# Retention in half chunks: q and k laid out over the partitions by halves, scores and state products in one stretch of TensorE, outputs in one stretch

## The chip, the core and the metric

The kernel runs on one core of a Trainium2 chip. The metric is the device time in microseconds (us), median of three runs. The engines are TensorE (PE, with its weight loads PEld), VectorE (DVE), ScalarE (ACT), GpSimd (POOL) and SyncE (SP), which issues all the loads and stores here.

## The reference

A retention layer (linear attention with a decay per head) feeds a two-layer network with an ELU. All is fp32.

```python
# q, k, v: (B, H, S, D) = (4, 8, 768, 64); gamma[h] = 1 - 2 ** (-5 - h)
for t in range(S):
    state = gamma * state + k[:, :, t] (outer) v[:, :, t]
    y[:, :, t] = scale * q[:, :, t] @ state
x = y.transpose(0, 2, 1, 3).reshape(3072, 512)
h = x @ w_in                                   # 512 -> 2048
out = where(h > 0, h, exp(min(h, 0)) - 1) @ w_out   # 2048 -> 512
```

Retention is a small part of the arithmetic; the two products with w_in and w_out are the rest.

## The kernel before

The 3072 tokens are cut into 24 chunks of 128 and these into 6 blocks (`tb`) of 512. For each block the kernel computes the retention of its 4 chunks, which gives x transposed in `xb`, and then two phases of the network: the first phase (x times w_in, with ELU into tiles `gC`, `gT`) and the second (times w_out). Block 0 uses plain products (`plain_first` L455, `plain_second` L483); later blocks use Strassen's scheme, partly twice nested (`first_twice` L733, `first_rest` L786, `second_twice` L813), with 128x128 and 128x256 matmuls whose sums and differences VectorE and ScalarE form. Some weights are decoded on VectorE during block 0 (`prepare` L140, `decode` L167), combined and stored to scratch memory, and fetched from there in the second phases (`fetch_small` L675).

The order of every engine's work is written out by hand: the program text interleaves the retention of block tb+1 with the phases of block tb. The function `retention_step` (L1065) is called at chosen places: in the main loop (L1127) steps 1 and 0 stand in the first phase (L1187, L1204) and steps 2 to 4 in the second (L1217). For block 2 all steps lie in block 1's second phase (L1121); for block 1 they lie between the matmuls of `plain_second` (L1046 to L1056); for block 0 everything is at the start (L983 to L1033), part by part as the loads land.

Retention works on half chunks of 64 tokens, `sub` = 0 or 1, and a state is a 64x64 matrix per head. Decay is folded into v (`scale_v` L258, on POOL for most chunks: v' = v times a factor per token and head) and into a factor per token at the end (`etab`). So a state is the plain running sum of k^T v', and the output of a half chunk is (masked scores) times v' plus q times the state in front of it. All these matmuls are 64x64x64: each uses one of four quarters of the PE array, given by the half of the partitions that the operands lie on (row half) and the half of the partitions of the output (column half).

Before the change q and k lie transposed, with the head pairs on the partition halves: tile `qk` is [64*a + d, q or k, head pair p, token of the chunk], head = 2p + a. Token-major k and v lie in `kvn` [token, k or v, head, d]. Then:

- `scores` (L299) computes the scores of two chunks: row half a (the head parity), column half sub, bank `sc[a]`. VectorE multiplies by the causal mask (L305) and writes into the k^T part of `qk`.
- `states` (L339): k^T v' of each half chunk in row half sub, column half a, bank `kvs[sub]`; `state_sum` (L330) adds it to the state before on VectorE (128 partitions x 256), or copies it on ScalarE where a sequence starts. States are kept in the place of k in `kvn`; the last of a block goes to `carry`.
- `outputs` (L348), a generator with pauses, accumulates y in two banks `y[sub]`. The products with the masked scores (L363) use row half sub. Those with the state (L389) use row half a, in two rounds: first where a = sub, then where a differs from sub. In the second round a row half writes into the bank that the other row half has just written, so two small reads of the banks on VectorE (`seen`, L377) stand between the rounds, and matmuls of the second wait for them. Then VectorE multiplies by `etab` into `xb` (L398).

Per block the 64x64 matmuls stand in five places of TensorE's order: all scores; all state products; L363 and the first round of outputs for chunks 0 and 1; the same for chunks 2 and 3; the second round of both.

The pool `ps_r` has four PSUM banks, taken in turn by `sc`, `kv`, `y` and two products of the first phase. The first phase's sums (`first_end` L799, add at L802) read PSUM on VectorE; TensorE then accumulates a further product into the same bank (L794).

Of the kernel before, what the change touches and what calls it, by code (L numbers as in the profile page):

```python
# [17 lines left out]
def kernel(  # L18
# [85 lines left out]
    def load_one(m, which, behind=None):  # L104
        if which == 0:
            raw[m] = [ldpool.tile([P, 2, HP, C], FP32, name="qk", tag="qk"), None]
            t = raw[m][0].rearrange("p a h c -> p (a h c)")
        else:
            raw[m][1] = ldpool.tile([C, 2, H, D], FP32, name="kvn", tag="kvn")
            t = raw[m][1].rearrange("p a h c -> p (a h c)")  # L110
        hold(t, behind)
        nc.sync.dma_start(t, qkv[m, :, 1024 * which : 1024 * which + 1024])
# [142 lines left out]
    carry = [const.tile([P, HP, D], FP32, name=f"carry{n}") for n in range(2)]  # L255
# [18 lines left out]
    def state(tb, n):  # L274

        if n % (2 * CPB) == 0:
            return carry[(tb + n // (2 * CPB)) % 2]
        if (tb, n) == (0, 3):

            return xt[0].rearrange("p a t -> p (a t)")[:, 0:256].rearrange("p (h e) -> p h e", e=D)  # L280

        k = raw[tb * CPB + (n - 1) // 2][1][:, 0].rearrange("p h d -> p (h d)")
        return k[:, (n - 1) % 2 * 256 : ((n - 1) % 2 + 1) * 256].rearrange("p (h e) -> p h e", e=D)
# [5 lines left out]
    def score_products(sc, tb, pp, x):  # L289
        qk = raw[tb * CPB + 2 * pp + x][0]  # L290
        for p in range(HP):
            for sub in range(2):
                for a in range(2):
                    nc.tensor.matmul(  # L294
                        sc[a][rows(sub), x, p, :], lhsT=qk[rows(a), 1, p, rows(sub)],
                        rhs=qk[rows(a), 0, p, rows(sub)], start=True, stop=True, skip_group_check=True,
                    )

    def scores(tb, pp):  # L299

        sc = [ps_r.tile([P, 2, HP, D], FP32, name="sc", tag="r") for _ in range(2)]
        for x in range(2):
            score_products(sc, tb, pp, x)
        for a in range(2):
            nc.vector.tensor_tensor(  # L305
                out=raw[tb * CPB + 2 * pp + a][0][:, 1].rearrange("p h c -> p (h c)").rearrange("p (n t) -> p n t", t=D),
                in0=sc[a].rearrange("p x h t -> p (x h) t"),
                in1=cmask.unsqueeze(1).to_broadcast([P, 2 * HP, D]), op=ALU.mult,
            )

    def mask_pair(sc, x):

        place = raw[x][0][:, 1].rearrange("p h c -> p (h c)").rearrange("p (a n t) -> p a n t", a=2, t=D)
        for a in range(2):
            nc.vector.tensor_tensor(
                out=place[:, a], in0=sc[a][:, x], in1=cmask.unsqueeze(1).to_broadcast([P, HP, D]), op=ALU.mult
            )

    def state_products(kvs, tb, pp, x, subs):
        kv = raw[tb * CPB + 2 * pp + x][1]  # L320
        for p in range(HP):
            for sub in subs:
                for a in range(2):
                    if not fresh(tb, 4 * pp + 2 * x + sub + 1):
                        nc.tensor.matmul(  # L325
                            kvs[sub][rows(a), x, p, :], lhsT=kv[rows(sub), 0, 2 * p + a, :],
                            rhs=kv[rows(sub), 1, 2 * p + a, :], start=True, stop=True, skip_group_check=True,
                        )

    def state_sum(kvs, tb, pp, x, sub):  # L330
        n = 4 * pp + 2 * x + sub
        if fresh(tb, n + 1):
            return
        if fresh(tb, n):
            nc.scalar.copy(state(tb, n + 1), kvs[sub][:, x])
        else:
            nc.vector.tensor_tensor(out=state(tb, n + 1), in0=kvs[sub][:, x], in1=state(tb, n), op=ALU.add)

    def states(tb, pp):  # L339

        kvs = [ps_r.tile([P, 2, HP, D], FP32, name="kv", tag="r") for _ in range(2)]
        for x in range(2):
            state_products(kvs, tb, pp, x, range(2))
        for x in range(2):
            for sub in range(2):
                state_sum(kvs, tb, pp, x, sub)

    def outputs(tb, pp, first=False):  # L348
# [6 lines left out]
        for x in range(2):  # L355
            kv = raw[tb * CPB + 2 * pp + x][1]
            for j in range(4):
                a, u = divmod(j, 2)
                pt = raw[tb * CPB + 2 * pp + (x if first else a)][0][:, 1].rearrange("p h c -> p (h c)")
                for sub in range(2):  # L360
                    for c in range(2):
                        p = 2 * u + c
                        nc.tensor.matmul(  # L363
                            y[sub][rows(c), j, x, :], lhsT=kv[rows(sub), 1, head(a, u, c), :],
                            rhs=pt[rows(sub), ((a if first else x) * HP + p) * D :][:, 0:D],
                            start=(x == 0 and j == 0), stop=False, skip_group_check=True,
                        )
            if first and x == 0:
                yield
        for other in range(2):  # L370
            if not other:
                yield
            else:

                for sub in range(2):
                    seen = epool.tile([P, 8], FP32, name="seen", tag="seen")
                    nc.vector.tensor_copy(seen.rearrange("p (j x) -> p j x", x=2), y[sub][:, :, :, 0])  # L377
                yield
            for x in range(2):
                q = raw[tb * CPB + 2 * pp + x][0]  # L380
                for u in range(2):
                    for a in range(2):
                        sub = a ^ other
                        n = 4 * pp + 2 * x + sub
                        if fresh(tb, n):
                            continue
                        for c in range(2):
                            p = 2 * u + c
                            nc.tensor.matmul(  # L389
                                y[sub][rows(c), 2 * a + u, x, :], lhsT=state(tb, n)[rows(a), p, :],  # L390
                                rhs=q[rows(a), 0, p, rows(sub)], start=False, stop=True, skip_group_check=True,
                            )
        if first:
            yield
# [8 lines left out]
    def outputs_step(tb, step):  # L403

        if step == 0:
            held["y"] = [outputs(tb, pp) for pp in range(2)]
        if step < 2:
            next(held["y"][step])
            next(held["y"][step])
        else:  # L410
            for g in held["y"]:
                next(g, None)
# [569 lines left out]

    unread(2, TB)  # L983
    sc = [ps_r.tile([P, 2, HP, D], FP32, name="sc", tag="r") for _ in range(2)]
    score_products(sc, 0, 0, 0)
    mask_pair(sc, 0)
    scale_v(0)
    unread(1, TH)
    kvs = [ps_r.tile([P, 2, HP, D], FP32, name="kv", tag="r") for _ in range(2)]
    state_products(kvs, 0, 0, 0, range(2))  # L990
    state_sum(kvs, 0, 0, 0, 0)
    state_sum(kvs, 0, 0, 0, 1)
# [5 lines left out]
    score_products(sc, 0, 0, 1)  # L998
    take(2)
    mask_pair(sc, 1)  # L1000
# [4 lines left out]
    state_products(kvs, 0, 0, 1, [0])  # L1005
    next(y)
    state_sum(kvs, 0, 0, 1, 0)
# [3 lines left out]
    next(y)  # L1011
    take(2)
    next(y)
    state_products(kvs, 0, 0, 1, [1])
# [3 lines left out]
    state_sum(kvs, 0, 0, 1, 1)  # L1018
# [6 lines left out]
    scores(0, 1)  # L1025
    states(0, 1)
# [19 lines left out]
    for n, _ in enumerate(plain_second()):  # L1046
        decode_all()
        prepare()
        if n == 1:
            scores(1, 0)  # L1050
            scores(1, 1)
        elif n == 2:
            states(1, 0)
            states(1, 1)
        elif 3 <= n <= 5:
            outputs_step(1, n - 3)  # L1056
        elif n == 6:
            for _ in combine_w_in(0):
                pass
# [3 lines left out]


    def retention_step(tb, step):  # L1065
        if tb >= NTB:
            return
        if step == 0:
            scores(tb, 0)
            scores(tb, 1)  # L1070
        elif step == 1:
            states(tb, 0)
            states(tb, 1)
        elif step < 5:
            outputs_step(tb, step - 2)
# [43 lines left out]
    for step, s in enumerate(sec):  # L1119
        if step in (0, 1, 2, 4, 5):  # L1120
            retention_step(2, (0, 1, 2, 2, 3, 4)[step])  # L1121
        if s == ORDER2[-1]:
            break
# [3 lines left out]
    for tb in range(2, NTB):  # L1127
# [86 lines left out]
        for step, s in enumerate(sec):  # L1214

            if step in (1, 3, 5):
                retention_step(tb + 1, 2 + step // 2)  # L1217
# [54 lines left out]
```

## Time and profile before

| what | value |
|---|---|
| device time, median of 3 runs | 648.82 us (647.68 to 651.66) |
| span of the profiled execution, first to last instruction | 645.3 us |
| PE busy | 634.9 us, 98% of the span |
| VectorE busy | 496.9 us, 77% |
| ScalarE busy | 240.8 us, 37% |
| POOL busy | 39.0 us, 6% |
| mean granted TensorE clock | 0.997 |
| scores L294: PE instructions, duration of one | 768, 218 ns |
| state products L325 | 704, 218 ns |
| products with masked scores L363 | 704 and 64 (block 0's first), 218 ns |
| mask L305, 128x512 | 22, 680 ns |
| state sum L337, 128x256 | 30, 425 ns (10 more in groups of other operands) |
| first state of a sequence, ScalarE L335, 128x256 | 4, 373 ns |
| `seen` L377, 128x8 | 24, 158 ns |
| outputs times etab L398, 128x512 | 24, 680 ns |

The profile is of one execution, of which only the span is recorded and no device time; the median of the runs is 3.5 us above the span. Matmuls of different array quarters overlap, and their ends are modelled, so the duration of one says little about the pace: that is read from when groups start. Idle time of an engine is given with what ended it; "issue" means that nothing in the profile explains it. A few records of matmuls are missing from the trace, so that counts in a stretch can be a little low.

In time, block 0's start and plain products take up to about 145 us of the span (the retention of block 1 at 94 to 131 us), block 1 up to about 250 us (the retention of block 2 at 199 to 242), and each of blocks 2 to 5 about 100 us.

### The profile page before, as it was taken

How to read it: one execution, taken by the hardware profiler on the slowest of the kernel's cores; microseconds unless marked ns; L12 is line 12 of the kernel's file. 1: busy time of each engine (PE TensorE's matmuls, PEld its weight loads, DVE VectorE, ACT ScalarE, POOL GpSimd, SP SyncE). 2: the span in 40 equal slices, each digit the busy share in tenths (PEclk: the TensorE clock that was granted, in tenths of full speed). 3: DMA queues.
4: the chain of work that ended last, by engine and by line, in shares of the span. 5: the costliest groups of instructions: out<-in, count | busy, mean ns of one | idle time of the engine just before them, and what ended most of it. 6: DMA issues, size and time to landing. Idle time of an engine off the chain costs nothing.

```text
span 645.3 us, 15896 instructions
## 1 busy us (share of the span) xinstructions
PE 634.9 (98%) x6526; PEld 542.7 (84%) x6526; DVE 496.9 (77%) x889; ACT 240.8 (37%) x463; POOL 39.0 (6%) x41
## 2 busy tenths in 40 slices
PE   7999999999999999999999999999999999999998
PEld 4774445548889999989999989999988999988998
DVE  4889799898979676589867488867569959557976
ACT  4577531204552112556111465211465311356311
POOL 1001100000460000100000110000020000000000
PEclk9999999999999999999999999999999999999999
DMA  8749777999488789802789920788840688710695
GB/s 302 288 136 369 267 236 213 319 272 258 150 282 268 211 262 316 294 5 56 245 278 289 306 87 16 223 275 286 292 171 3 197 263 264 226 49 1 212 313 162
DMA packets 85209, 139.72 MB, mean 217 GB/s; under 512 B 6672, under 2 KB 38800, under 8 KB 82832
## 3 DMA queue, kind: packets, MB, share of 16 engines
q1 hardware_dynamic: 85136, 138.70, 66.5%
q8 instruction: 52, 0.85, 0.5%
q14 instruction: 21, 0.17, 0.1%
HBM read 114.56 MB, written 24.12 MB: 215 GB/s over the span
## 4 chain that ended last, share of the span: by engine, by line
PE 69%; DVE 7%; DMA 2%; POOL 1%; issue 1%; SPq 1%; ACT 1%; POOLq 0%; DVEq 0%
PE pa L833 20%; PE pa L794 10%; PE pd L833 9%; PE pb L833 5%; PE pa L748 4%; PE pb L794 4%; PE qa L794 3%; PE pd L748 2%; PE qd L794 2%; PE pd L794 2%; POOL wi L699 1%; PE y L363 1%; PE y L389 1%; PE sc L294 1%; PE kv L325 1%
## 5 line engine op out<-in xcount | busy, mean ns | idle before, releaser
L841 ACT COPY ms<-pa 128x128 f32<-128x128 f32 x104 | 27.7, 266 | 147.0 <-PE pa L833 145.5
L833 PE MATMUL pa<-ts,wq 128*128 128x128 f32 x560 | 74.0, 275 | 0.3 <-ACT ms L841 0.3
L833 PE MATMUL pd<-ts,wq 128*128 128x128 f32 x552 | 73.2, 275 | 0.0
L833 PEld LDWEIGHTS pa<-ts,wq 128*128 128x128 f32 x560 | 68.5, 192 | 0.8 <-ACT ms L841 0.5
L833 PEld LDWEIGHTS pd<-ts,wq 128*128 128x128 f32 x552 | 67.1, 192 | 0.3 <-DVE res L845 0.2
L833 PE MATMUL pa<-gC,wq 128*128 128x128 f32 x480 | 64.7, 278 | 0.0
L444 ACT ACTIVATE r<-r 128x512 f32<-128x512 f32 x96 | 60.5, 630 | 3.1
L833 PEld LDWEIGHTS pa<-gC,wq 128*128 128x128 f32 x480 | 59.0, 192 | 1.3
L443 ACT ACTIVATE r<-gC 128x512 f32<-128x512 f32 x64 | 39.9, 624 | 32.0 <-DVE gC L802 32.0
L845 DVE TENSOR_TENSOR res<-pd,ms 128x128 f32<-128x128 f32 x68 | 19.5, 287 | 37.0 <-PE pd L833 35.8
L268 POOL TENSOR_TENSOR kvn<-kvn,vf 128x512 f32<-128x512 f32 x21 | 24.9, 1189 | 330.7 <-DMA kvn<-in_qkv_dram 226.1
L447 DVE SCALAR_TENSOR_TENSOR gC<-r,gC 128x512 f32<-128x512 f32 x64 | 42.5, 696 | 0.7 <-ACT r L444 0.7
L710 DVE TENSOR_TENSOR ts<-gC,ts 128x512 f32<-128x512 f32 x60 | 41.3, 688 | 1.0
L710 DVE TENSOR_TENSOR ts<-gC 128x512 f32<-128x512 f32 x60 | 41.0, 683 | 0.0
L833 PE MATMUL pb<-gC,wq 128*128 128x128 f32 x240 | 32.8, 277 | 0.1
L490 PE MATMUL pa<-gC,w_s 128*128 128x512 f32 x64 | 30.6, 600 | 0.0
L833 PEld LDWEIGHTS pb<-gC,wq 128*128 128x128 f32 x240 | 29.5, 192 | 0.8 <-DVE gC L447 0.8
L866 ACT COPY res<-pa 128x128 f32<-128x128 f32 x34 | 9.0, 266 | 56.3 <-PE pa L833 56.3
L802 DVE TENSOR_TENSOR gC<-qa,gC 128x512 f32<-128x512 f32 x8 | 5.5, 692 | 25.1 <-PE qa L794 18.3
L574 ACT COPY m<-pa 128x512 f32<-128x512 f32 x24 | 13.9, 580 | 25.6 <-PE pa L794 14.4
L794 PE MATMUL pa<-xt,w_s 128*128 128x256 f32 x96 | 23.0, 382 | 0.0
L794 PE MATMUL pa<-xt,w_b 128*128 128x256 f32 x96 | 23.0, 382 | 0.0
(224 smaller groups left out, 1239.6 us busy)
## 6 DMA issues: line engine op xcount, KB each, us to landing
wq<-scratch_dram SPq DMA_DIRECT2D x277, 256.0 KB, 4.3
wraw<-in_w_dram SPq DMA_DIRECT2D x16, 1024.0 KB, 6.3
qk<-in_qkv_dram SPq DMA_DIRECT2D x24, 512.0 KB, 6.6
kvn<-in_qkv_dram SPq DMA_DIRECT2D x24, 512.0 KB, 7.3
scratch_dram<-w_s SPq DMA_DIRECT2D x8, 512.0 KB, 4.9
scratch_dram<-so SPq DMA_DIRECT2D x8, 512.0 KB, 4.8
out_dram<-res SPq DMA_DIRECT2D x14, 256.0 KB, 3.8
scratch_dram<-gT SPq DMA_DIRECT2D x12, 256.0 KB, 4.3
```

Of the source, the lines that this page charges most:

```text
L268: eng.tensor_tensor(out=kv[:, 1], in0=kv[:, 1], in1=vf[:, i].unsqueeze(2).to_broadcast([C, H, D]), op=ALU.mult)
L443: nc.scalar.activation(e, h, AF.Relu, scale=-1.0)
L444: nc.scalar.activation(e, e, AF.Exp, scale=-1.0)
L447: nc.vector.scalar_tensor_tensor(g, e, -1.0, h, ALU.add, ALU.max)
L490: nc.tensor.matmul(ops[d], lhsT=wo[:, row, (d if row else d ^ 2) * P :][:, 0:P], rhs=g_plain[row * NF + f], start=(n == 0 and row == 0), s ...
L574: nc.scalar.copy(m, ps)
L710: sub = lambda o, x, y: nc.vector.tensor_tensor(out=o, in0=x, in1=y, op=ALU.subtract)
L748: nc.tensor.matmul(ps[:, f, :], lhsT=lhs[f], rhs=xs[j][k], start=(begin and f == 0), stop=True, skip_group_check=True,)
L794: nc.tensor.matmul(ps[:, fi, :], lhsT=w[:, fi, j2, :], rhs=x[:, j2, :], start=(j in (1, 7) and fi == 0 and j2 == 0), stop=(j2 == 1), skip_ ...
L833: nc.tensor.matmul(ps, lhsT=w[:, f, :], rhs=ts[j][k][:, f, :], start=(begin and f == 0), stop=(f == 3), skip_group_check=True,)
L841: nc.scalar.copy(m, ps)
L845: nc.vector.tensor_tensor(out=o, in0=x, in1=y, op=ALU.add)
```

## The change

The host lays out q and k by half chunks: tile `qk` becomes [64*sub + d, q or k, head, token of the half chunk]. Row half sub then holds half chunk sub for all heads. From this follow:

- Scores of half chunk sub use row half sub and column half sub, in one bank `sc` per chunk. State products use row half sub and column half 1 - sub, in one bank `kv` per chunk. `scores_states` issues them in turn, head by head, for two chunks in one stretch, then the masks (one of 128x512 per chunk), then the sums.
- A state lies on one half of the partitions, all heads side by side: state n on half n % 2. A sum is 64 partitions x 512. The state at the end of a block is first kept in `kvn` and copied to `carry` by ScalarE when the outputs of the block are finished.
- In `outputs` the products with the state also use row half sub, so each bank `y[sub]` is written by one row half only. The second round, the `seen` reads and the pauses around them are gone. Both pairs of chunks are issued in one stretch.
- `retention_step` has four steps in place of five: 0 and 1 are `scores_states` of two chunks each, 2 issues all outputs with the multiplications of the first pair, 3 the multiplications of the second pair. In the main loop steps 0 and 1 keep their places in the first phase, and 2 and 3 stand at `step` 3 and 4 of the second phase, where the old steps stood at 1, 3 and 5.
- In block 0, chunks 0 and 1 are still computed part by part: scores of one chunk in one stretch and its state products in another.

```diff
-            raw[m] = [ldpool.tile([P, 2, HP, C], FP32, name="qk", tag="qk"), None]
+            raw[m] = [ldpool.tile([P, 2, H, D], FP32, name="qk", tag="qk"), None]
...
-    carry = [const.tile([P, HP, D], FP32, name=f"carry{n}") for n in range(2)]
+    carry = const.tile([P, H, D], FP32, name="carry")
...
+        r = rows(n % 2)
+        if n == 0:
+            return carry[r]
...
+        return raw[tb * CPB + (n - 1) // 2][1][r, 0]
...
+    def score_product(sc, m, h):
+        qk = raw[m][0]
+        for sub in range(2):
+            nc.tensor.matmul(
+                sc[rows(sub), h, :], lhsT=qk[rows(sub), 1, h, :], rhs=qk[rows(sub), 0, h, :],
+                start=True, stop=True, skip_group_check=True,
             )
...
+    def state_product(kvs, tb, i, h, subs):
+        kv = raw[tb * CPB + i][1]
+        for sub in subs:
+            if not fresh(tb, 2 * i + sub + 1):
+                nc.tensor.matmul(
+                    kvs[rows(1 - sub), h, :], lhsT=kv[rows(sub), 0, h, :], rhs=kv[rows(sub), 1, h, :],
+                    start=True, stop=True, skip_group_check=True,
+                )
+
+    def mask(sc, m):
+
+        nc.vector.tensor_tensor(
+            out=raw[m][0][:, 1], in0=sc, in1=cmask.unsqueeze(1).to_broadcast([P, H, D]), op=ALU.mult
+        )
+
+    def state_sum(kvs, tb, i, sub):
+        n = 2 * i + sub
+        if fresh(tb, n + 1):
             return
+        new = kvs[rows(1 - sub)]
         if fresh(tb, n):
-            nc.scalar.copy(state(tb, n + 1), kvs[sub][:, x])
+            nc.scalar.copy(state(tb, n + 1), new)
         else:
-            nc.vector.tensor_tensor(out=state(tb, n + 1), in0=kvs[sub][:, x], in1=state(tb, n), op=ALU.add)
...
+            nc.vector.tensor_tensor(out=state(tb, n + 1), in0=new, in1=state(tb, n), op=ALU.add)
...
+    def scores_states(tb, pp):
+
+        both = [(2 * pp + x, by_heads("sc"), by_heads("kv")) for x in range(2)]
+        for i, sc, kvs in both:
+            for h in range(H):
+                score_product(sc, tb * CPB + i, h)
+                state_product(kvs, tb, i, h, range(2))
+        for i, sc, kvs in both:
+            mask(sc, tb * CPB + i)
+        for i, sc, kvs in both:
             for sub in range(2):
-                state_sum(kvs, tb, pp, x, sub)
+                state_sum(kvs, tb, i, sub)
...
-                for sub in range(2):
-                    seen = epool.tile([P, 8], FP32, name="seen", tag="seen")
-                    nc.vector.tensor_copy(seen.rearrange("p (j x) -> p j x", x=2), y[sub][:, :, :, 0])
-                yield
...
+        for x, j, sub, c in places:
+            i, h, o = at(x, j, sub, c)
+            n = 2 * i + sub
+            if not fresh(tb, n):
+                nc.tensor.matmul(
+                    o, lhsT=state(tb, n)[:, h, :], rhs=raw[tb * CPB + i][0][rows(sub), 0, h, :],
+                    start=False, stop=True, skip_group_check=True,
+                )
+        yield
+        if pp == 1 and not fresh(tb, 2 * CPB):
+            nc.scalar.copy(carry[rows(0)], state(tb, 2 * CPB))
...
         if step == 0:
             held["y"] = [outputs(tb, pp) for pp in range(2)]
+            for g in held["y"]:
+                next(g)
+                next(g)
+            next(held["y"][0], None)
+        else:
+            next(held["y"][1], None)
+
+    def retention_step(tb, step):
+        if tb >= NTB:
+            return
         if step < 2:
-            next(held["y"][step])
-            next(held["y"][step])
+            scores_states(tb, step)
         else:
-            for g in held["y"]:
-                next(g, None)
+            outputs_step(tb, step - 2)
...
-        if n == 1:
-            scores(1, 0)
-            scores(1, 1)
-        elif n == 2:
-            states(1, 0)
-            states(1, 1)
-        elif 3 <= n <= 5:
-            outputs_step(1, n - 3)
+        if 1 <= n <= 4:
+            retention_step(1, n - 1)
...
-        if step in (0, 1, 2, 4, 5):
-            retention_step(2, (0, 1, 2, 2, 3, 4)[step])
+        if step in (0, 1, 3, 4):
+            retention_step(2, (0, 1, None, 2, 3)[step])
...
-            if step in (1, 3, 5):
-                retention_step(tb + 1, 2 + step // 2)
+            if step in (3, 4):
+                retention_step(tb + 1, step - 1)
...
-        x.reshape(B, H // 2, 2, NC, C, D).transpose(0, 3, 2, 5, 1, 4).reshape(B * NC, 128, H // 2 * C) for x in (q, k)
+        x.reshape(B, H, NC, 2, C // 2, D).transpose(0, 2, 3, 5, 1, 4).reshape(B * NC, 128, H * C // 2) for x in (q, k)
```

## Prediction

> **What bounds the kernel now.** I read the page first, then the chain of waits of the whole run and of single stretches, then the timelines of VectorE and TensorE around the retention work. "Position" means one of the four 64x64 quarters of the array, "visit" one stretch of 64x64 matmuls between stretches of full 128-row matmuls. Counts of PE are instructions; an fp32 matmul is two of them.
>
> ```profile
> PE 634.9 (98%) x6526; PEld 542.7 (84%) x6526; DVE 496.9 (77%) x889; ACT 240.8 (37%) x463; POOL 39.0 (6%) x41
> ```
>
> TensorE is busy 98% of the span of 645.3 us, and the timeline shows it at full pace almost everywhere after 20 us. The chain of the whole run, at a visit of the first phase (columns: start, length, what):
>
> ```profile
> 281.21 2.02 PE sc L294 x128
> 283.23 1.92 PE pa L794 x8
> 285.16 1.73 PE pb L794 x8
> ```
>
> The chain of the stretch 300 to 350 us, at the first outputs visit of the second phase:
>
> ```profile
> 311.31 0.89 PE pa L833 x8
> 312.20 1.09 PE y L363 x64
> 313.30 0.47 PE y L389 x22
> 313.76 1.09 PE pa L833 x8
> 314.85 0.89 PE pb L833 x8
> ```
>
> 64 instructions take 1.09 us and 128 take 2.02, so one costs (2.02 - 1.09) / 64 = 14.5 ns and the way in 1.09 - 64 x 0.0145 = 0.16 us. The first full-size group behind a visit takes 1.09 in place of 0.89, or 1.92 in place of 1.73: the way out is 0.20. A visit costs 0.36 us beside its work. The 32 in the middle (0.47 us; some records are missing) pay no way in. In the visit L325 at 387.31, 16 of 128 are left out (all of one chunk's second half) and it still takes 2.01: each position keeps a pace of 4 x 14.5 = 58 ns, and only four positions in use give 14.5.
>
> One more loss lies in a visit (chain of 195 to 255 us):
>
> ```profile
> 217.59 0.45 PE y L389 x26
> 218.03 1.21 issue
> 219.24 0.34 PE y L389 x6
> ```
>
> TensorE stands 1.21 us inside the first outputs visit of block 2, for nothing the profile names.
>
> VectorE is the second resource. Its timeline in block 5's first phase:
>
> ```profile
> 489.46 1.34 DVE L337 TENSOR_TENSOR kvn<-kv,kvn 128x256 f32<-128x256 f32 x3
> 491.00 1.34 DVE L337 TENSOR_TENSOR kvn<-kv,kvn 128x256 f32<-128x256 f32 x3 [0.20 <-DVE kvn L337]
> 492.26 0.68 DVE L802 TENSOR_TENSOR gC<-pa,gC 128x512 f32<-128x512 f32 x1
> 492.86 0.68 DVE L802 TENSOR_TENSOR gC<-pa,m 128x512 f32<-128x512 f32 x1
> 493.46 0.68 DVE L802 TENSOR_TENSOR gC<-pa,gC 128x512 f32<-128x512 f32 x1
> 495.14 0.69 DVE L802 TENSOR_TENSOR gC<-pb,m 128x512 f32<-128x512 f32 x1 [1.00 <-PE pb L794]
> ```
>
> and that of TensorE beside it:
>
> ```profile
> 494.94 1.89 PE L794 MATMUL pa<-xt,w_s 128*128 128x256 f32 x8
> ```
>
> From 482.08 to 494.14 VectorE has almost no gap. The add at 493.46 reads the bank into which TensorE accumulates at 494.94: it has 0.80 us to spare. The same place has 0.84 in block 4 (393.70 against 394.54, and 0.44 idle just before) and 0.56 in block 3 (293.73 against 294.29).
>
> At the end of block 1 VectorE is late already:
>
> ```profile
> 148.72 1.96 PE L624 MATMUL pa<-xt,w_s 128*128 128x256 f32 x8 [0.57 <-DVE xt L417]
> ```
>
> [...] Today each row half has its own bank; no run shows the changed pattern. [...] L337 425, L305 680. So half the partitions with twice the elements costs more.
>
> **The change part by part.**
>
> *Matmuls.* Their number stays. Scores use the positions (0,0) and (1,1), k^T v' uses (0,1) and (1,0), in turn, each in its own bank. Four positions stay in use, so 128 instructions per visit at 14.5 ns. Unknown: whether two row halves writing different halves of one bank slow down. From nothing up to two positions at a time, 29 ns; I take nothing, because the partitions are disjoint.
>
> *Visits.* Per block of 512 tokens five become three: two of 128 stay two, three of outputs (96, 96, 64) become one of 256. Two times 0.36 = 0.72 us per block, and blocks 2 to 5 lie where TensorE sets the pace: -2.9.
>
> *The stall of 1.21 us.* It falls in a visit that moves one step later and changes its instructions. It may vanish or come back elsewhere: 0 to -1.2, I take -0.6.
>
> *`seen` and the split outputs.* Two copies of 155 ns and their wait go. Around block 0 the wait held TensorE 0.3 us twice; later none. The work of L389 follows L363 directly.
>
> *State sums.* 128x256 becomes 64x512. In a dependent chain one starts 0.435 us after the other now (489.46 to 491.00, gaps aside; block 4: five from 388.53 to 390.74). A dependent pair of 128x512 (L710, 192.73 and 193.44) gives 0.71. So +0.275 each, 6 or 7 on VectorE per block: +1.65 to +1.9. Half of them, with two masks, follow the first visit, the rest the second; masks cost the same, one of 128x512 per chunk. The copy that starts a sequence on ScalarE grows from 0.37 to some 0.59 (L574, 128x512). One copy of the carry per block is new there, 0.59, behind outputs, where ScalarE is busy 8.0 of 46 us (304 to 350); without that cover it would hold up a copy `ms` that TensorE needs, 0.5 per block at most.
>
> Where the extra VectorE time ends: behind the sums are the adds L802, and for the third of them waits TensorE. Block 5: masks and sums of step 0 1.24 + 4 x 0.71 = 4.1 for 2.5 now, step 1 3.4 for 3.3: the add ends 1.65 later at 495.8, TensorE waits 0.9. Block 4: three sums a step, +0.9 and +0.7, less 0.44 idle: 394.9, a wait of 0.4. Block 3: +0.9 and +0.4: 295.05, a wait of 0.8. Together +2.1. All of TensorE's work queues behind that L794; VectorE's own lateness ends there, since it has 1.0 us free ahead of 495.14. The second phase has VectorE gaps of 0.4 to 1.8 us (315.85, 317.57, 330.11): the outputs' multiplications, now 1.3 twice in place of 2.5 once, cost nothing there; without the gaps they would cost 1.3 per block.
>
> In block 2 both visits lie in the second phase. There step 0 grows by 1.6, ahead of L653 (done at 208.0, read by TensorE at 209.9): 1.9 to spare, nothing lost.
>
> *Waits that the order adds.* k^T v' of chunks 0 and 1 comes one step earlier and needs v' from POOL: L268 has them at 369.9, the visit starts at 381.6; chunks 2 and 3 at 376.7 for 387. A visit takes all four banks of ps_r, so the second needs the sums of the first: in block 5 these end at 483.29 + 4.1 = 487.4, and the bank read last is written from 487.65 + 0.16 + 0.93 = 488.7. Both free, with 10 and 1.3 us to spare. No DMA is moved.
>
> *Ahead of 190 us.* In block 0 chunks 0 and 1 are computed apart, so scores use two positions and k^T v' two or one: up to 0.47 us more for each of four stretches, twice that at half clock. Those of chunk 0 hide under the 2.1 us wait for the DMA of the next qk (L294 at 12.11); those of chunk 1 do not, but `seen` leaves the same chain: +0.3. Then 1.4 us more of sums lie ahead of the decoded weights that L465 reads at 32.15: +0.45. In block 1 sums add 1.65 to a full VectorE, and the first multiplications of outputs move ahead of 119.5, where SP's queue waits for VectorE and the stores L527 begin that free the buffers at 127 and 131.9; 2.5 us of multiplications leave 136.4 in return. The last weights are ready at 138.5 to 139.2 in place of 136.5, while TensorE reads them at 137.67. The two visits saved there (0.7) are lost again to this. I take +0.5 for all of it, from -1 to +1.5.
>
> The sum: -2.9 - 0.6 + 2.1 + 0.5 = -0.9 us on a span of 645.3, so 644.4. The runs' median, 648.82, lies 3.5 above the span and moves alike: 648.0.
>
> **The rivals.**
>
> *A, VectorE's lateness is absorbed* (22%). For: only one bank's reuse has too little slack. Against: 12 us without a gap ahead of it. Then all that is saved stays: 0.72 x 5 blocks, 1.2 of the stall, 0.3 of `seen`: -5.1, 643.7.
>
> *B, VectorE's lateness spreads* (14%): every first phase loses 2 us in place of 0.7 and the weights of block 1 arrive 2 later: 3 x 1.3 + 1.5 over my sum, about 653.
>
> *C, slower* (9%): in the visits of scores and states the two row halves in one bank exclude each other. The pace is then 29 ns: 1.86 us more in each of 10 visits, 648.0 + 18.6 = 667. It decides from some 20 ns on: (6.5 + 0.8) / 1280 instructions = 5.7 ns over 14.5 makes 1% slower. Against it: the disjoint partitions.
>
> *D, faster by over 1%* (4%): it needs 6.5 us, more than all visits and stalls named; only if the longer visits remove waits I do not see.
>
> My own case has 51%, with 646 to 650 as its range.
>
> **How the numbers follow.** About 1%, 6.5 us, is what a measurement of this kernel can tell from no change. Own case, A and most of B are within it: 0.84; slower is C and the tail of B: 0.12; faster 0.04. The range runs from A's 643.7, a little under, to B's 653: it leaves out C, D and the tail of B.
>
> **What would show it.** Right: three visits per block, of 128, 128 and 256 instructions in 2.0, 2.0 and 3.9 us; sums of about 0.68; a wait of PE for DVE L802 of 0.4 to 0.9 us in the first phases of blocks 3 to 5; gaps of blocks between 200 and 550 us shorter by about nothing. Wrong: visits of scores over 2.6 us (C); no wait for L802 (A); TensorE reaching 190 us over 1.5 us later or 1 us earlier than now; a stall inside the visit of 256.

## The result, and the profile after the change

The changed kernel takes 666.31 us (median of 4 runs, 661.89 to 667.1) where the kernel before, on the same chip, takes 648.25 (645.56 to 651.66): ratio 1.0265, 95% interval 1.0211 to 1.0318. It is slower. The profiled execution took 665.81 us with a span of 664.0, 18.7 more than before.

Where the 18.7 us lie comes from the moments at which TensorE starts the same product in both traces:

| stretch | before, us | after, us | difference |
|---|---|---|---|
| up to the second phase of block 1 | 190.70 | 189.06 | -1.6 |
| second phases with retention work (four) | 198.13 | 213.43 | +15.3 |
| first phases with retention work (three) | 149.71 | 154.77 | +5.1 |
| everything else | 106.79 | 106.78 | 0.0 |

The waits of TensorE over the whole run (what waits, for what: us in total, times, longest) name the new losses:

```profile
PE y L361 <- issue: 8.0, 4, 2.6
PE pa L775 <- DVE gC L783: 4.0, 3, 1.5
PE y L350 <- issue: 2.7, 1, 2.7
PE pd L814 <- DVE res L826: 2.5, 6, 1.2
```

"issue" is time in which the engine waited for nothing that the profile shows. It is 10.7 us now, all of it inside the outputs' visits (L350 is scores times v', L361 the states); in the kernel before there was one such wait, of 1.21 us. The two others are waits for VectorE: the one foreseen (L783 is the line called L802 before), and one that was not (L826).

The chain of waits of the stretch 300 to 340 us, the outputs' visit of block 3:

```profile
328.38 1.09 PE y L350 x64
329.47 0.93 PE y L361 x45
330.39 1.31 issue
...
331.92 0.95 PE y L350 x64
332.87 0.93 PE y L361 x63
333.80 1.64 issue
...
335.65 1.09 PE pa L814 x8
```

The work itself keeps its pace, 64 pairs of weight load and matmul in 0.93 us. But TensorE stands twice, and between the two stands it runs 128 pairs: 256 instructions. The same visit in blocks 2, 4 and 5 has one stand of 2.6 to 2.7, 2.58 and 2.48 us. It lasts 6.7 to 7.3 us where 3.9 were predicted. In block 1 the same visit of 240 pairs takes 3.90 us without a stand.

The table of DMA queues says what there are 256 of (packets, MB, share of the time):

```profile
q8 instruction: 52, 0.85, 0.5%
```

52 packets of 16 KB carry TensorE's own instructions: its 6526 weight loads, 6526 matmuls and 267 others (semaphores nearly all) are 52.0 times 256, so 64 bytes each and 256 in a packet. Counted along the trace, all five stands of the changed kernel and the one of the kernel before lie at the same place of this count, behind the 193rd instruction after a multiple of 256. I take this place for the border between two packets. The visit of block 1 fits this: the packet that it needs at its border, pair 127, had begun to arrive 5 us before the visit (106.4 against 111.4 us).

In block 5 the stand is followed by something else:

```profile
541.84 2.48 issue
544.32 1.65 PE y L361 x49
545.97 2.00 PE pa L814 x8
547.97 1.71 PE pb L814 x8
```

After it everything takes about twice its time (8 matmuls of L814 took 0.89 before). The granted clock between 544.3 and 551.1 us is 0.53; this costs 3.2 us more.

And the scores and states of block 3, whose two row halves now write into one bank (stretch; busy us and instructions of TensorE; granted clock; DMA share; GB/s):

```profile
282.94:284.97 2.03, 2.03 (x130) 1.00 0.01 4
```

2.03 us, as before; over all blocks 2.02 to 2.15.

### The profile page after: what moved, and what is told of

It is laid out like the page before. It is cut to its first block, busy times and chain, and to the rows that moved or that the text cites. A ratio compares the mean times of both kernels' runs of the same rounds, so it can differ in the third digit from the quotient of the medians.

```text
span 664.0 us, 15881 instructions
## 1 busy us (share of the span) xinstructions
PE 638.9 (96%) x6526; PEld 547.1 (82%) x6526; DVE 505.1 (76%) x863; ACT 243.6 (37%) x467; POOL 39.9 (6%) x41
## 4 chain that ended last, share of the span: by engine, by line
PE 56%; DVE 19%; issue 4%; DMA 2%; POOL 1%; ACT 1%; SPq 0%; DVEq 0%; POOLq 0%
PE pa L814 14%; PE pd L814 8%; PE pa L775 7%; PE pa L729 4%; PE pb L814 4%; DVE ts L691 4%; PE qa L775 3%; DVE kvn L320 3%; PE pb L775 3%; PE pd L729 2%; PE qd L775 2%; PE pd L775 2%; DVE res L826 2%; DVE gC L634 1%; DVE gC L428 1%
## 5 line engine op out<-in xcount | busy, mean ns | idle before, releaser
L814 PE MATMUL pd<-ts,wq 128*128 128x128 f32 x552 | 74.2, 278 | 2.5 <-DVE res L826 2.5
L814 PE MATMUL pa<-ts,wq 128*128 128x128 f32 x560 | 74.1, 276 | 0.3 <-ACT ms L822 0.3
L814 PEld LDWEIGHTS pd<-ts,wq 128*128 128x128 f32 x552 | 67.1, 192 | 4.6 <-DVE res L826 4.5
L814 PEld LDWEIGHTS pa<-ts,wq 128*128 128x128 f32 x560 | 68.6, 192 | 0.8 <-ACT ms L822 0.5
L814 PE MATMUL pa<-gC,wq 128*128 128x128 f32 x480 | 65.0, 279 | 0.0
L814 PEld LDWEIGHTS pa<-gC,wq 128*128 128x128 f32 x480 | 59.9, 194 | 2.7 <-issue 1.9
L826 DVE TENSOR_TENSOR res<-pd,ms 128x128 f32<-128x128 f32 x68 | 19.5, 286 | 36.0 <-PE pd L814 33.9
L428 DVE SCALAR_TENSOR_TENSOR gC<-r,gC 128x512 f32<-128x512 f32 x64 | 45.5, 735 | 1.6 <-ACT r L425 0.9
L814 PE MATMUL pb<-gC,wq 128*128 128x128 f32 x240 | 33.6, 282 | 0.1
L826 DVE TENSOR_TENSOR res<-pb,ms 128x128 f32<-128x128 f32 x36 | 10.3, 285 | 28.2 <-PE pb L814 28.1
L471 PE MATMUL pa<-gC,w_s 128*128 128x512 f32 x64 | 30.5, 598 | 0.7 <-DVE w_s L187 0.7
L814 PEld LDWEIGHTS pb<-gC,wq 128*128 128x128 f32 x240 | 30.4, 197 | 0.8 <-DVE gC L428 0.8
L292 PEld LDWEIGHTS sc<-qk 64*64 64x64 f32 x768 | 24.1, 135 | 6.4 <-issue 4.1
L301 PE MATMUL kv<-kvn 64*64 64x64 f32 x704 | 27.6, 221 | 1.2 <-DVE kvn L268 0.8
```

The source lines that it names most:

```text
L301: nc.tensor.matmul(kvs[rows(1 - sub), h, :], lhsT=kv[rows(sub), 0, h, :], rhs=kv[rows(sub), 1, h, :], start=True, stop=True, skip_group_ch ...
L428: nc.vector.scalar_tensor_tensor(g, e, -1.0, h, ALU.add, ALU.max)
L471: nc.tensor.matmul(ops[d], lhsT=wo[:, row, (d if row else d ^ 2) * P :][:, 0:P], rhs=g_plain[row * NF + f], start=(n == 0 and row == 0), s ...
L814: nc.tensor.matmul(ps, lhsT=w[:, f, :], rhs=ts[j][k][:, f, :], start=(begin and f == 0), stop=(f == 3), skip_group_check=True,)
L826: nc.vector.tensor_tensor(out=o, in0=x, in1=y, op=ALU.add)
```

## The experiments

Two theories stand against each other for the 10.7 us of stands. **S, supply**: TensorE runs 256 small instructions in 1.86 us, faster than the next packet of instructions arrives. **L, layout**: the stands are waits for data or a bank, made by the new places of q, k and the states. A third theory, **V**, is about the first phases: the longer state sums on VectorE hold up the add that TensorE waits for.

### Two visits of outputs in place of one

```diff
-        if step == 0:
-            held["y"] = [outputs(tb, pp) for pp in range(2)]
-            for g in held["y"]:
-                next(g)
-                next(g)
-            next(held["y"][0], None)
-        else:
-            next(held["y"][1], None)
+        for _ in outputs(tb, step):
+            pass
```

> The changed kernel, but the outputs of the two pairs of chunks in two visits (128 instructions at step 3, 128 at step 4) in place of one of 256; layout, sums and all else as changed. Theory S (instruction supply: TensorE's instructions come in packets of 16 KB, 256 instructions; a visit of 256 pairs of weight load and matmul is 512 of them, runs them in 3.7 us and outruns the next packet): the four visits' stalls of 8.0 + 2.7 = 10.7 us go, at most one of up to 2.5 us stays where a packet's border falls so that a whole packet lies in one visit, the slow clock behind the stall of block 5 (2.4 us) goes, 4 x 0.36 us of visits come back: 666.3 - 10.7 - 2.4 + 1.4 = 654.6; if VectorE's lateness in the second phases came from the long visit too, up to 1 us less per block: 650 to 656. Rival L (the stall is a wait for data or for a bank, made by the new layout): the stalls stay, in the visits of 128, time 664 to 668.

657.21 us, ratio to before 1.0145 (1.0099 to 1.0191); the kernel before had 647.1 beside it. So 9 us come back, less than expected and outside the range: three of the eight visits still stand, 4.3 us in all, and behind the one of block 2 the granted clock is 0.50 from 236.00 to 239.41 us, which costs another 1.7. Their borders lie at pairs 101 (block 2), 111 (block 3) and 95 (block 4). The chain at the one of block 3:

```profile
330.62 0.93 PE y L361 x45
331.55 1.31 issue
332.86 0.21 PE y L361
```

The first phases are as long as in the changed kernel (51.8, 51.2, 51.8). The visit's length matters, as S says; but a visit of 128 is not short enough when a border falls near its end.

### The kernel before, with two of its visits merged

```diff
         if step == 0:
             held["y"] = [outputs(tb, pp) for pp in range(2)]
-        if step < 2:
-            next(held["y"][step])
-            next(held["y"][step])
-        else:
+            for g in held["y"]:
+                next(g)
+                next(g)
+        elif step == 2:
             for g in held["y"]:
                 next(g, None)
```

> The kernel before, with only the first two of its three visits of outputs put together (96 + 96 = 192 pairs at step 1, the last 64 at step 5 as they were); old layout, old sums. Theory S: the borders of the packets of 256 instructions fall 90 pairs into block 2's long visit, 100 into block 3's, 77 into block 4's, 61 and 189 into block 5's. Only block 5's holds a whole packet: a stall of about 2.5 us there near pair 189, up to 1.2 in block 2 (the old one) and up to 0.5 in blocks 3 and 4; 4 x 0.36 us are saved: 648 to 652. Rival L (the new layout makes the stalls): no stall but perhaps the old one in block 2, 646 to 648.

648.2 us in one run, span 646.4. Block 2 stands at pair 89, 1.3 us, and block 5 has a new stand of 1.9 us. It comes 7 matmuls behind the visit, since the border lies there (200 pairs from the visit's start, counted in the instruction list) and not at pair 189, where I had put it from the trace. One more, of 3.1 us, lies in block 0, on a border too, where nothing was changed:

```profile
515.43 0.98 PE pa L833 x7
516.40 1.90 issue
518.31 0.27 PE pa L833
```

The packet that ends here holds the visit's last 120 pairs. Old layout, old sums, and an ordinary full-size matmul that stands: L alone doesn't explain it. In blocks 3 and 4 there is no stand, as S expected.

### Every border moved by half a packet

```diff
     unread(1, TB)
+    for n in range(32):
+        r = rows(n % 2)
+        nc.tensor.matmul(
+            warm[r, 0:D], lhsT=blank[r, 0:D], rhs=blank[r, 0:D], start=True, stop=True, skip_group_check=True
+        )
     sc = by_heads("sc")
```

> The changed kernel, with 32 small matmuls of zeros more near the start, where TensorE waits for a DMA: 64 weight loads and 64 matmuls, 128 instructions, half a packet. Nothing else changes, so every border between packets falls 64 pairs earlier in the visits after it. Theory S: the stalls move with it: in block 2 from pair 160 to 224 (96 + 128), in block 3 from 111 and 239 to 175, in block 4 from 223 to 159, in block 5 from 207 to 143, each 2.5 us or so, since the packet ahead of them then lies whole in the visit; time 664 to 668. Rivals: a wait for data or a bank stays at its pair (160, 111 and 239, 223, 207); a throttle stays at its time after the start of the visit (2.3 us in block 2, 1.6 and 3.5 in block 3, 3.2 and 3.0).

672.19 us in one run. The stands moved with the borders, as S said, and none stayed at its pair or its time: block 3 stands once, at pair 175, block 4 at 159, block 5 at 143, block 2 at 96 (2.2 us between starts) and 224 (0.5), and block 1, which had none, now stands 4.45 us at pair 191. In block 2 the long stand came at the earlier of the two borders, which I had not expected. The time lies above the range of S; behind four of the stands the granted clock is 0.50 for 3.41 us, 6.8 us lost in all where the changed kernel lost 3.2. Block 3 in the chain:

```profile
338.57 0.93 PE y L350 x58
339.49 2.34 issue
341.83 0.21 PE y L350
```

The line that stands is now L350 in place of L361: the operation doesn't matter, the count of instructions does. This settles S against L and against a throttle as the cause of the stands.

### The supply by itself

A kernel of its own: `full(64)`, then `visit(pairs)`, for 128, 192, 256 and 512 pairs of zeros, twice.

> A kernel of its own, without the reference's work (its outputs are zeros): stretches of 64 full-size matmuls (256 instructions) and between them visits of 128, 192, 256 and 512 pairs on four 64x64 positions, first with no DMA under way, then with 24 MB of loads in 96 transfers running. Borders between packets of 256 instructions fall at pairs 31 and 159 in the visits of 128 and 192, at 95, 223, 351 and 479 in the others. Theory S: in the quiet half the visits of 128 have no stall; the visit of 256 stalls once, about 2 us at pair 223, that of 512 three times, at pairs 223, 351 and 479, each so that a packet's period is 3.5 to 3.7 us against 1.86 us of work. Under load the same borders stall, longer, up to 5 us a period, and those of the shorter visits may stall too. Rival Q: the packet is late only because of the loads: no stall in the quiet half, a visit of 512 in 7.6 us.

The visit of 512 in the quiet half, from the chain of waits:

```profile
141.42 3.42 PE y L33 x223
144.84 1.09 issue
145.93 2.09 PE y L33 x128
148.02 1.64 issue
149.66 2.09 PE y L33 x128
151.75 1.64 issue
```

From 145.93 to 149.66 are 3.73 us for 128 pairs, to 153.38 once more 3.72. That is 256 instructions, 14.6 ns each, supplied without any other DMA. The visits of 128 took 2.02 us without a stand, those of 256 stood 1.3 and 1.1 us between starts, and that of 192, which I had not listed, 1.7. So Q falls: it is no matter of loads alone. The loads ran only from about 185 to 255 us, so of the second half just the visits of 128 and 192 lay under them. The first had no stand; the second:

```profile
232.97 2.48 PE y L33 x159
235.46 3.55 issue
```

Here the packet began 3.1 us after the border before it had been crossed, in place of 1.2 in the quiet half. One pair of visits shows this. It fits the second phases of the real kernels: the packet that ends a stand begins 0.8 to 6.2 us after the border before it where the DMA engines were over 0.6 busy in between, and 1.0 us in the two stands where they were 0.10 busy. The packet takes 0.9 to 1.2 us, and TensorE goes on 1.2 to 1.7 us after its end.

### Half the state sums

```diff
-            nc.vector.tensor_tensor(out=state(tb, n + 1), in0=new, in1=state(tb, n), op=ALU.add)
+            few = slice(0, H // 2 if tb > 1 else H)
+            nc.vector.tensor_tensor(
+                out=state(tb, n + 1)[:, few], in0=new[:, few], in1=state(tb, n)[:, few], op=ALU.add
+            )
```

> The changed kernel, with VectorE's state sums of blocks 2 to 5 cut from 64x512 to 64x256 (the sums of the upper four heads are left out, so their carried states are not those of the reference). Takes 0.27 us from each dependent sum, about what the layout added. Theory V (the waits of PE L775 for the add DVE gC L783, 1.5, 1.0 and 1.5 us in the first phases of blocks 3 to 5, come from these sums): they go to under 0.3 each, the stalls inside the outputs' visits stay at about 10.7 in all: 660 to 663. Rival: the waits stay, since two masks and four sums now follow the first visit at once, whatever their length: 664 to 667.

658.5 us (655.91 to 661.34), ratio 1.0185 (1.0127 to 1.0244). The waits for the add are gone from the list, the first phases take 50.0, 49.9 and 50.0 us (49.9 in the kernel before), 4.8 less in all; the stands are still there (10.4 us, at pairs 160, 239, 223 and 207). V holds. The time fell by 7.8 rather than some 5, more than the range of V. Two more things differ between the profiled runs: the waits for `res` in the second phases are 1.0 us in place of 2.5, and the clock stays full behind block 5's stand but is 0.50 from 226.66 to 230.07 us, at the end of block 2's, so that it costs at most 1.7 in place of 3.2.

### Scores and states of chunks 2 and 3 moved to the second phase

```diff
-            if n == 2 and more:
-                retention_step(tb + 1, 1)
...
-            if step in (3, 4):
-                retention_step(tb + 1, step - 1)
+            if step == 2 and more:
+                held["sums"]()
+            elif step in (1, 3, 5):
+                retention_step(tb + 1, 1 + step // 2)
```

> The kernel of two visits of outputs (128 each), and the scores and states of chunks 2 and 3 moved out of the first phase: visit and masks to step 1 of the second phase, its sums to step 2, the outputs to steps 3 and 5. Nothing is left out. Theory V: the waits of PE for the add DVE gC in the first phases (4.0 us) go, first phases of 49.9 us in place of 51.2 to 51.8. Theory S: three visits of 128 pairs now lie in each second phase, with borders between packets at pairs 100 (block 3, scores), 110 (its first outputs), 8 and 136 (its second), 92 and 102 (block 4's outputs); where a packet holds over 90 pairs of a visit, 1 to 2.5 us each, 5 to 8 us in all. Together 649 to 655. Rival (what is lost lies in the layout itself): no better than the two visits, 656 to 659.

650.73 us, ratio 1.0054 (1.0034 to 1.0073). The waits for the add fall from 4.0 to 0.2 us with all sums complete. The first phases last 47.7, 47.7 and 48.1: 2.2 less than before is the visit that left. The stands, 5.1 us by the rows of issue, lie at borders at pairs 100, 110, 82, 103 and 74.

### The same with visits of 64

Scores and states of chunks 2 and 3 at step 0, sums at step 1, each pair's outputs in two visits:

```diff
-        for _ in outputs(tb, step):
-            pass
+        if step % 2 == 0:
+            held["y"] = outputs(tb, step // 2)
+            next(held["y"])
+        else:
+            for _ in held["y"]:
+                pass
```

> As the one before, but scores and states of chunks 2 and 3 at step 0 of the second phase, their sums at step 1, and the outputs of each pair in two visits of 64 (scores times v' first, states next) at steps 2 to 5: the changed layout with neither a long visit nor a full VectorE in the first phase. Nothing is left out. Theories S and V together: no wait for the add in the first phases, no stall in a visit of 64, at most 1 to 2 us each in the three visits of scores and states at steps 0 (borders at pairs 32, 16 and 112); six visits per block in place of five before, 4 x 0.36 us more: 647 to 652, so the whole loss of the change is accounted for. Rival (a third cause): 655 or more.

652.46 us, ratio 1.0093 (1.007 to 1.0116). No visit of the second phases stands, and the first phases wait for VectorE by 0.2 us at most. What is left is the second phase's VectorE, which gets the sums while it makes the next product's inputs:

```profile
PE pd L818 <- DVE res L830: 5.2, 4, 1.8
```

So I bought the stands off at a price: 5.2 us of this wait, one visit per block more than before, and 1.7 us at half clock behind the longest of the waits. The time is a little above the range, and under the 655 of the rival. What is left is neither S nor V: it is VectorE's second phase, to which my expectation gave no price, the same omission as in the prediction.

### The kernel before, borders moved

28 such small matmuls of zeros, ahead of the scores of chunk 1 in the kernel before.

> The kernel before with 28 small matmuls of zeros more near the start, where TensorE waits for a DMA: 112 instructions, which move every border between packets of 256 instructions 56 pairs earlier. Nothing else is changed. In the kernel before one border falls 90 pairs into the first outputs visit of block 2 (96 pairs) and TensorE stands 1.21 us there. Theory S: the border now falls at pair 34 of that visit, behind a stretch of slow instructions, and at pairs 78 and 76 of the visits beside it; the stall goes and none takes its place: 1.2 us less, ratio 0.998, 644.5 to 646 where the kernel before has 646.2. Rival W (that stall is a wait for data or a bank of this visit): it stays, ratio 1.000.

646.85 us, ratio 0.9989 (0.9966 to 1.0011). The interval holds both 0.998 and 1.000, so the time decides nothing and the traces must. The stand at the first outputs visit of block 2 is gone, so W falls. But another came, at the border in the visit of the states before it:

```profile
206.71 1.31 PE kv L325 x77
208.02 1.69 issue
```

That packet began only 6.2 us after the border before it was crossed, and the stretch between them, 51 pairs of full-size work and 77 small, was shorter than the supply. A second one, 1.5 us, at the border behind block 3's second outputs visit coincides with a wait for a DMA. My claim that none would take its place was wrong: the border can be counted, the delay of a packet can't.

No version of the changed layout beats the kernel before. The best of them, with the later scores, has a span of 651.1 us; without its 5.1 us of stands and 1.7 at half clock it would be at 644.3 by my estimate. The kernel before, 645.3, without its own stand of 1.2 and 1.7 at half clock would be at 642.4.

## Why the prediction was wrong, step by step

*The visits.* Right in number, wrong in what a visit is worth. Three visits per block, 128, 128 and 256, in 2.0 to 2.15, 2.0 to 2.1 and, for the last, 6.7 to 7.3 us. **The step that failed** is the cost of the visit of outputs, 256 times 14.5 ns and 0.36: the pace was taken from visits of 64 and 128, which mostly ran without a stand (2.02 us for 128 pairs in the kernel made for the supply). A visit of 256 stands: in that kernel long visits get 128 pairs per 3.73 us. The saving of 0.36 per visit is real: with merged visits and no stand, the kernel before has second phases of 46.64 us in blocks 3 and 4, and 47.00 without the merging. But -2.9 is small beside +9.5 of stands, from 1.2 to 10.7.

*The stall of 1.21 us.* The prediction had it on the page and priced it from 0 to -1.2, as something that could only go. It was the one sample of the mechanism, and the change then made five stands of one and 10.7 us of 1.2. The place said it: 90 pairs into a visit, nothing named, a full-size stretch before. An unexplained stand in the very operation that the change makes longer needed a price upwards too. I named "a stall inside the visit of 256" as what would show the prediction wrong, and gave it no chance.

*The half clock.* Not foreseen: 3.2 us behind block 5's stand. In the traces of this case the stretches at half clock lie on a grid of 3.41 us, whose place differs from run to run: in the kernel before the clock changes at 13.62, 17.03 and 645.08 us (the last two are 184 times 3.413 apart), in the changed kernel at 543.90, 550.73 and 663.37 (2 and 33 times). I took TensorE's idle time in each period of this grid that ran at full clock, some 1800 in ten traces. All 17 periods with 1.87 us or more were followed by half clock, none with 1.79 or less was, and of two with 1.84 one was. So it is chance which stand meets it: of block 5's 2.48 us, 2.06 fell into one period (540.49 to 543.90), while block 2's 2.69 were split into 0.85 and 1.84, and block 4's 2.58 into 0.93 and 1.64; both were followed by full pace.

*The state sums and the first phases.* Right in mechanism and place, too small: 5.1 us by the phases' lengths where 2.1 were predicted. Half the sums take 4.8 of it away. In block 5 VectorE's timeline gives the size, first before the change (its last sums end at the L802 of 492.26, shown in the prediction):

```profile
483.29 2.48 DVE L305 TENSOR_TENSOR qk<-sc,cmask 128x512 f32<-128x512 f32 x4
485.68 0.68 DVE L447 SCALAR_TENSOR_TENSOR gC<-r,gC 128x512 f32<-128x512 f32 x1
...
488.94 0.42 DVE L337 TENSOR_TENSOR kvn<-kv,carry 128x256 f32<-128x256 f32 x1
```

then after it:

```profile
494.52 1.50 DVE L308 TENSOR_TENSOR qk<-sc,cmask 128x512 f32<-128x512 f32 x2
496.06 0.69 DVE L320 TENSOR_TENSOR kvn<-kv,carry 64x512 f32<-64x512 f32 x1
...
499.11 0.69 DVE L428 SCALAR_TENSOR_TENSOR gC<-r,gC 128x512 f32<-128x512 f32 x1
...
502.38 1.28 DVE L308 TENSOR_TENSOR qk<-sc,cmask 128x512 f32<-128x512 f32 x2
503.69 1.41 DVE L320 TENSOR_TENSOR kvn<-kv,kvn 64x512 f32<-64x512 f32 x2
...
506.03 0.69 DVE L783 TENSOR_TENSOR gC<-pa,gC 128x512 f32<-128x512 f32 x1
...
507.24 0.68 DVE L783 TENSOR_TENSOR gC<-pa,gC 128x512 f32<-128x512 f32 x1
```

and TensorE's the wait:

```profile
507.98 2.00 PE L775 MATMUL pa<-xt,w_s 128*128 128x256 f32 x8 [1.53 <-DVE gC L783]
```

The masks and sums of step 0 take from 494.52 to the next work at 499.11, 4.59 us where I had 4.1; those of step 1 take 502.38 to 506.03, 3.65 for 3.4. Together 8.24 against 5.7 before (2.39 and 3.32), 2.5 later and not 1.65. One sum costs 0.71 to 0.73 from start to start, as predicted. The seven sums with their gaps take 5.39 in place of 3.32, 2.07 more where 1.65 to 1.9 was taken, and the masks 2.85 in place of 2.39, where I had taken no difference: the first group takes 1.50, since it starts while its visit still runs. With 0.80 to spare that leaves 1.7; the trace has 1.53. In block 3 the prediction also misread the time to spare: the chain has TensorE's products there from 294.29 on, its timeline has the first of them start at 294.12, so 0.39 us and not 0.56. Its own sum would then have been +2.3.

*The second phases on VectorE.* Priced at nothing for its gaps: wrong. Of the +15.3 us there 9.5 are stands and 3.2 the clock, visits give back 2.9, and 5.5 are left. The waits for L826, 2.5 us, are the part that the profile names. 1.8 of them are in the second phase with block 2's retention, where masks and sums of step 0 come before the adds `res` that TensorE needs and I had written "nothing lost". In blocks 3 and 4 VectorE idles through the long visit (5.09 us behind `pb`, at 337.74) and then has a product's inputs and the outputs' multiplications in one heap. The gaps I had counted on lie elsewhere once the visit is one piece. The remaining 3.0 us were not taken apart; some of it is the end of each stand, which takes 0.2 more from start to start than its row of issue says.

*Ahead of 190 us.* A gain of 1.6 where +0.5 (from -1 to +1.5) was taken: the first product with decoded weights begins at 17.82 in place of 19.78, behind the scores of chunk 1, which had their qk at 10.39 rather than 12.11. This gain isn't shown to be the change's. Behind its 2.1 us wait for that qk the kernel before ran at a granted clock of 0.50 from 13.62 to 17.03 us, which costs 1.7; the changed kernel had 1.00 there. With 28 small matmuls in that wait (the run with borders moved), the kernel before had 1.00 too, and reached the product of the table's first row at 188.98, the changed kernel at 189.06. And with two of its visits merged, which changes nothing so early, it had its qk at 10.46. The wait for the weights at the end of block 1 came as foreseen (0.7 us, L471 for `w_s`), and the old one for `xt` went.

*The rivals.* C's number, 667, is almost the measured one, by accident. That the disjoint partitions would keep the pace was an assumption of the prediction; the changed kernel showed it, and so refuted C: two row halves in different partitions of one bank keep 14.5 ns per instruction, 2.03 us for 128. A is refuted by the waits for L783. B came near for the first phases, with 2 us each where 1.7 were measured, and did not name the cause of the larger loss. D has nothing for it.

## What to carry to other kernels

Merging short stretches of small matmuls saved the way in and out, 0.36 us per visit here, but the longer stretches ran ahead of their instructions, 1.86 us of work against 3.73 of supply for 128 pairs: visits of 128 pairs mostly ran free, and visits of 240 or 256 never did in a second phase. Look for an "issue" wait that repeats at a distance of 256 instructions, count the instructions of the change before merging, and keep full-size work between small visits. And a wait with no name that sits inside the operation a change enlarges is to be priced in both directions.

## What the runs showed of the hardware that was not expected

- In the visit of 512 pairs, without other traffic, TensorE's instructions arrived at 256 in 3.73 us (14.6 ns each); pairs of load and matmul on four 64x64 positions used two of them every 14.5 ns (64 pairs in 0.93 us). Full-size matmuls took 14.2 us for 256 instructions by the pace of L814 (8 pairs in 0.89 us); where they stood, it was just behind a visit (1.9 us, with two visits of the kernel before merged).
- A packet whose lateness made TensorE stand began 0.6 to 1.2 us after the border before it where the DMA engines were at most 0.10 busy in between, and, in the second phases of the real kernels, 0.8 to 6.2 us after it where they were over 0.6 busy.
- The half clock came in stretches of 3.41 us (13.62 to 17.03 in the kernel before) or twice that (543.90 to 550.73 in the changed one), each beginning behind a period of the trace's grid in which TensorE had been idle for 1.84 us or more (1.9 and 2.06 in these two); in the changed kernel one with 1.84 (226.46 to 229.88) was followed by full clock. A stand of 1.9 us was enough (block 4's first, with the later scores: 1.87 in one period), and one of 3.03 was not (block 5 with half the sums: split into 1.79 and 1.24).
